# A SwiGLU kernel with its steady block written out in a new order

## The chip, the cores and the metric

The kernel runs on one core of a Trainium2 chip. The metric is the device time of one execution in microseconds (us). A core has TensorE for matrix products (PE in the profile, its weight loads PEld), VectorE (DVE), ScalarE (ACT), GpSimd (POOL) and SyncE (SP), which here only issues DMA transfers. Each engine works through its own instructions in the order in which the program wrote them; an instruction that waits holds up all that stands behind it on its engine.

## The reference

The input is x, 8 sequences of 4096 tokens with 192 channels. It goes through a causal convolution with 7 taps, whose weights are a softmax per head (8 heads of 24 channels), and then through a normalised SwiGLU layer with 1536 hidden channels. Cut to what matters:

```python
w = np.exp(w - np.max(w, axis=-1, keepdims=True))          # weight: 8 heads x 7 taps
w = w / (np.sum(w, axis=-1, keepdims=True) + 1e-09)
out = np.einsum('hk,bskhg->bshg', w, x_unf)                # x_unf: the 7 last tokens
rms = np.sqrt(np.mean(x * x, axis=-1, keepdims=True) + 1e-06)
xn = x / rms * rms_g                                       # x: 32768 tokens x 192
g = xn @ w_gate                                            # 192 x 1536
silu = g * (1.0 / (1.0 + np.exp(-g)))
val = xn @ w_val                                           # 192 x 1536
return (silu * val @ w_out).astype(np.float32)             # 1536 x 192
```

## The kernel before

**Blocks.** The 32768 tokens are cut into 32 pairs of two groups of 512 tokens. The first two pairs are computed with plain products while the weights are still being prepared. Pairs 2 to 31 use a scheme of seven sums and products in place of eight products (Strassen's, in the form of Winograd), both for the gate and value products and for the output product. One steady block of the program is one such pair. It is written out by hand: there is no planner, and no loop decides an order.

**The lists.** The tuple LINE gives the order of the work on TensorE in a block: 68 products, then 42 output steps. The tuple ORDER gives, for the blocks 3 to 32, what all engines do: a word `pN` takes the next N entries of LINE, and each other word adds one instruction (or a few) to the engine of its first letter (A is ACT, V is DVE, G is POOL, S a DMA on the queue of SP). `-` behind a word means the pair before, `+` the next pair, `++` the one after that. SECOND is the same for pair 2, beside which pair 1 ends. FIRST is the same for pair 1; in it `W` takes the next turn of the weight preparation and `R` starts the ring of weights. The function `run` at the end of the kernel reads the words, `Pair.do` and `ahead` write the instructions.

**A product** (`Pair.product`, line 948) multiplies a weight piece with the normalised tokens or with sums of them. Numbers are split into three parts, and a product is six matrix instructions: three parts, each for the gate (first bank of a bank pair) and the value (second bank). The names are P1 to P7, Q1 to Q4 and A, B, E with a letter, then a point and a number j from 0 to 5, which says which sixth of the hidden channels is meant. The even and odd j do not have the same form: 0, 2, 4 and 5 use P and Q words, 1 and 3 use A, B and E words for four quarters a, b, c, d and no sums. The weight pieces lie in DRAM and stream through a ring of 12 slots: when the last product that uses a slot has been issued, the next load into it is put on the queue of SP (`ring_load`, line 822).

**Banks.** Four bank pairs of the accumulator memory (PSUM) are shared by all. For the j of the P and Q form, the scheme gathers the quarters in this order: P1, Q1 and P2 make quarter a; `f1.j` (ACT, line 705) copies a to the bank pair of b; P6, P7, Q3 and P4 add to it to give b; P5 opens the bank pair of c, `f3.j` (ACT, line 705) copies c to a place in the on-chip memory (tt), and `f4.j` and `f5.j` (DVE, line 1025) write the sums for c and d, to which P3, Q2 and Q4 add. So a product can stand behind a copy: P6 or P7 behind f1, P7 or Q3 behind f4 or f5, and a product that opens a bank pair behind the instruction that gives that pair free. For j = 5 (the constant APART) Q4.5 opens the fourth bank pair itself, and `f5.5` and `f6.5` (DVE, line 1018) add from it and from b. For each quarter, `ga.j` to `gd.j` (ACT, line 1031) take the silu of the gate, and `ma.j` to `md.j` (DVE, line 1038) multiply it with the value into the tiles ht; after that the bank pair is free.

**Hidden sums and output steps.** `h1.j` to `h4.j` (line 1003, on DVE as `Vh` or POOL as `Gh`) form the sums over the four quarters; h1 goes into hs, the others overwrite quarters in ht. An output step `oK.j` (`Pair.step`, line 976) multiplies one of these with form K of the output weights, in twelve small matrix instructions, gathered in bank pairs named X, Y and Z. `c1`, `s7` and `c2` (ACT, line 705) copy gathered results, `C22` and `C21` (DVE, line 1055) add them, `T11`, `T12`, `T21` and `T22` (DVE, line 991) transpose the four results into the tile o_sb, and `st` (SP, line 1087) stores it. The steps of form 3 stand behind C22, since they go on in the bank pair that C22 reads; the bank pairs of an old block come free with T11, T12 and C21, and the next block's first products open them.

**What a block does for later blocks.** `ld` loads tokens (line 174), `cv0` (ACT, line 470) and `cv1` to `cv6` (DVE, line 474, called taps here) are the convolution, `sq` squares (ACT, line 485), `red` sums over channels (DVE, lines 496 to 498), `pow` makes the factor (POOL, lines 503 to 509), `bc` spreads it (DVE, line 516), `mul` scales the tokens (POOL, line 524), `pl` puts them away to DRAM (line 1098), `ft` fetches them back transposed (line 676). `x1` to `x4` (line 868) are sums of the tokens, and `n`, `l` and `d` (lines 705, 856, 854) are the three parts of an operand.

**The preparation of weights** runs beside pair 1. `prepare(o)`, for ten kinds o of weight, is a row of stages: a difference (POOL, line 785), the high part (DVE, 788), a scaled copy (ACT, 793), the middle part that reads the copy (DVE, 795), a difference (POOL, 799), the last part (ACT, 801) and the store to DRAM (SP, 805). `turn_of(o, n)` says which o take their next stage in turn n; the turns are sorted by `45 * o + at` with a fixed list of at.

The lines that say how a word moves TensorE on, and when a slot of the ring is filled anew:

```python
if word[0] == "p":
    for _ in range(int(word[1:].rstrip("+-"))):
        if p in pairs:
            next(pairs[p].line)
...
left_of[key] -= 1
if left_of[key] == 0:
    ring_load(slot)
```

Of the kernel before, what the change touches and what calls it, by code (L numbers as in the profile page):

```python
# [20 lines left out]
def kernel(  # L21
# [58 lines left out]
    )  # L80
    ORDER = (
# [15 lines left out]
    )  # L97
    SECOND = (
# [15 lines left out]
    )  # L114
    FIRST = (
# [14 lines left out]
    )  # L130
    LINE = (
# [7 lines left out]
    )  # L139

    cst = ctx.enter_context(tc.tile_pool(name="cst", bufs=1))
# [1127 lines left out]

    def turn_of(o, n):  # L1270
        mine = (
            [o] * (o < 2), [o] * 2 * (o == 0), [o + 1, o, o + 1], [o, o + 2], [o], [o],
        )[n]
        for o in mine:
            if o < NW:
                next(makers[o], None)

    ready = iter([functools.partial(turn_of, o, n) for _, o, n in steps])
    put(base - 1, lambda: outer(first_hts, base))
    put(base + 445, functools.partial(next, pieces["t"], None))  # L1280
# [74 lines left out]
```

## Time and profile before

| what | before |
|---|---|
| median of 3 runs | 2460.54 us (2460.39 to 2461.25) |
| profiled execution | 2460.79 us |
| its span, first to last instruction | 2459.0 us |
| granted clock of TensorE | 1.000 |
| busy: PE, PEld | 2442.9 us (99%), 1886.5 us (77%) |
| busy: DVE, ACT, POOL | 2125.0 us (86%), 1024.3 us (42%), 487.9 us (20%) |
| DMA | 430.55 MB, mean 175 GB/s |

The span is counted from the first instruction to the last, and the profiled execution's own time is 1.8 us longer. Busy times are those of each engine alone. The chain is followed back from the last instruction, at each step to what released it. In a timeline, a row has the start, the duration, the engine, the line, the operation, what it writes and reads, its shape and the number of instructions that the row gathers; a bracket tells how long the engine was idle before and what released it. A row of the windows has, in this order, the stretch, its length, and the busy time with the number of instructions of PE, PEld, DVE, ACT and POOL, then the granted clock, the busy share of the DMA engines and their GB/s; where the row is that of one line, the first two numbers are PE and PEld of that line. A row of the waits has the engine, the line, who released it, the waiting time in all, how often, and the longest.

### The profile page before, as it was taken

To read this page: it belongs to the slowest core of one execution; us is meant where nothing else is said; L and a number is where in the kernel's file an instruction comes from. 1 tells how busy PE (TensorE), PEld (TensorE's weight loads), DVE (VectorE), ACT (ScalarE), POOL (GpSimd) and SP (SyncE) were. 2 spreads that over 40 slices of the span, in tenths; PEclk is the share of its full clock that TensorE was granted. 3 is DMA by queue.
4 is the path that set the end of the run, shared out by engine and by line. 5 is a ranking of instruction groups with operands and counts; after the bars stand their busy time and mean duration, and the time that the engine had idled before them with its cause. 6 is when DMAs were issued, how large, how long until landed. Compare 5 with 4: busy or idle time off the path is not lost.

```text
span 2459.0 us, 69164 instructions
## 1 busy us (share of the span) xinstructions
PE 2442.9 (99%) x29136; PEld 1886.5 (77%) x29136; DVE 2125.0 (86%) x2762; ACT 1024.3 (42%) x1431; POOL 487.9 (20%) x422
## 2 busy tenths in 40 slices
PE   8999999999999999999999999999999999999998
PEld 5647777877777777777777778777777777777776
DVE  8678888899888898888898888998888988888975
ACT  6443344443344443444443444433444434344432
POOL 0542222210222201222202222102222012222021
PEclk9999999999999999999999999999999999999999
DMA  7374778666777667777677786667776766776753
GB/s 152 61 213 125 178 182 212 186 166 168 177 192 206 169 176 175 178 201 200 157 176 176 179 214 184 168 168 180 187 209 168 178 175 178 197 201 160 177 162 92
DMA packets 716392, 430.55 MB, mean 175 GB/s; under 512 B 510330, under 2 KB 702386, under 8 KB 716082
## 3 DMA queue, kind: packets, MB, share of 16 engines
q1 hardware_dynamic: 712336, 425.21, 67.1%
q8 instruction: 230, 3.77, 0.7%
q10 hardware_dynamic: 3746, 0.92, 0.2%
q14 instruction: 80, 0.66, 0.1%
HBM read 366.96 MB, written 58.98 MB: 173 GB/s over the span
## 4 chain that ended last, share of the span: by engine, by line
PE 96%; DMA 1%; DVE 1%; SPq 1%; POOL 0%; ACT 0%; issue 0%; DVEq 0%; ACTq 0%; POOLq 0%
PE ps L948 58%; PE ps L976 36%; PE ps L1135 2%; PE ps L920 1%; DMA ht<-in_moe_w_val_dram 0%; DMA wd<-part 0%; SPq L174 0%; DMA x<-in_x_dram 0%; DVE part L795 0%; POOL part L799 0%; DMA ht<-in_moe_w_gate_dram 0%; DVE ht L1038 0%; SPq L258 0%; DVE ht L1003 0%; DVE part L788 0%
## 5 line engine op out<-in xcount | busy, mean ns | idle before, releaser
L948 PE MATMUL ps<-part,ring 64*128 64x512 f32 x11190 | 1322.7, 389 | 1.8 <-DVE o_sb L991 0.8
L948 PEld LDWEIGHTS ps<-part,ring 64*128 64x128 f32 x11190 | 1039.9, 184 | 250.8 <-DVE ps L1025 22.5
L1031 ACT ACTIVATE tt<-ps 128x512 f32<-128x512 f32 x744 | 438.6, 598 | 659.0 <-PE ps L948 472.8
L1038 DVE TENSOR_TENSOR ht<-ps,tt 128x512 f32<-128x512 f32 x744 | 501.7, 684 | 99.9 <-ACT tt L1031 98.4
L976 PE MATMUL ps<-ht,wo_sb 128*32 128x384 f32 (+2 forms) x7272 | 462.6, 380 | 0.0
L976 PE MATMUL ps<-ht,x 128*32 128x256 f32 (+2 forms) x6696 | 431.7, 379 | 0.0
L1003 POOL TENSOR_TENSOR hs<-ht 128x512 f32<-128x512 f32 x120 | 154.8, 1290 | 1270.6 <-DVE ht L1038 1270.6
L976 PEld LDWEIGHTS ps<-ht,wo_sb 128*32 128x32 f32 x7272 | 330.8, 110 | 98.0 <-DVE ps L1018 10.6
L976 PEld LDWEIGHTS ps<-ht,x 128*32 128x32 f32 x6696 | 299.0, 110 | 87.0
L1025 DVE TENSOR_TENSOR ps<-ps,tt 128x1024 f32<-128x1024 f32 x210 | 258.7, 1232 | 109.0 <-PE ps L948 88.1
L474 DVE SCALAR_TENSOR_TENSOR y<-xh,tp,y 128x1536 f32<-128x1536 f32 x186 | 337.5, 1815 | 1.6 <-ACT y L470 1.3
L705 ACT COPY tt<-ps 128x384 f32<-128x384 f32 (+1 forms) x182 | 151.6, 833 | 260.2 <-PE ps L976 230.5
L1003 DVE TENSOR_TENSOR ht<-ht 128x512 f32<-128x512 f32 x282 | 193.4, 704 | 22.6 <-PE ps L976 22.3
L705 ACT COPY ps<-ps 128x1024 f32<-128x1024 f32 (+1 forms) x151 | 134.0, 887 | 160.6 <-PE ps L976 106.7
L705 ACT CAST part<-tt 128x1024 fp32r<-128x1024 f32 x60 | 63.0, 1049 | 238.0 <-DVE tt L868 238.0
L1003 DVE TENSOR_TENSOR ht<-hs,ht 128x512 f32<-128x512 f32 x181 | 125.3, 693 | 23.8 <-PE ps L976 21.7
L976 PE MATMUL ps<-hs,x 128*32 128x128 f32 (+2 forms) x2232 | 131.6, 379 | 0.0
L976 PEld LDWEIGHTS ps<-hs,x 128*32 128x32 f32 x2232 | 96.5, 110 | 28.7
L948 PE MATMUL ps<-part,part 64*128 64x512 f32 x822 | 116.9, 388 | 0.0
L1003 POOL TENSOR_TENSOR ht<-ht 128x512 f32<-128x512 f32 x90 | 115.1, 1291 | 0.0
L503 POOL TENSOR_SCALAR r<-r 128x8 f32<-128x8 f32 x31 | 6.1, 197 | 524.6 <-DVE r L498 524.4
L856 DVE SCALAR_TENSOR_TENSOR part<-part,xb 128x1024 fp32r<-128x1024 f32 x87 | 106.1, 1219 | 0.0
(137 smaller groups left out, 1582.3 us busy)
## 6 DMA issues: line engine op xcount, KB each, us to landing
ring<-wd SPq DMA_DIRECT2D x1317, 192.0 KB
xb<-xd SPq DMA_DIRECT2D x60, 512.0 KB
part<-wd SPq DMA_DIRECT2D x123, 192.0 KB
xd<-xh SPq DMA_DIRECT2D x240, 96.0 KB
xh<-in_x_dram SPq DMA_DIRECT2D x192, 105.0 KB
xb<-xd SPq DMA_DIRECT2D x60, 256.0 KB
out_dram<-o_sb SPq DMA_DIRECT2D x126, 96.0 KB
out_dram<-o_sb SPq DMA_DIRECT2D x62, 128.0 KB
```

Source lines behind the costliest of these rows:

```text
L474: nc.vector.scalar_tensor_tensor(out=y, in0=xk, scalar=w, in1=y, op0=ALU.mult, op1=ALU.add)
L503: nc.gpsimd.tensor_scalar(out=r, in0=r, scalar1=s / D, scalar2=s * 1e-6, op0=ALU.mult, op1=ALU.add)
L705: nc.scalar.copy(out=dst, in_=src)
L856: nc.vector.scalar_tensor_tensor(out=split_of(g, 2).bitcast(F32R), in0=high, scalar=1.0 + SPLIT, in1=src, op0=ALU.mult, op1=ALU.subtract,)
L920: nc.tensor.matmul(out=self.both(j, c)[:, h, :], lhsT=wf[HALF[h], k, 2 * HOME[j] + f, :], rhs=rb[HALF[h], k, g, :], start=(k == 0), stop=( ...
L948: nc.tensor.matmul(out=self.both(j, c)[:, h, :], lhsT=left[HALF[h]], rhs=right[HALF[h]], start=(first and q == 0), stop=True, skip_group_c ...
L976: nc.tensor.matmul(out=self.acc(b)[i * Q : (i + 1) * Q, at : at + n], lhsT=left, rhs=cols, start=fresh, stop=True, skip_group_check=True, ...
L1003: engine[eng].tensor_tensor(out=dst, in0=a, in1=b, op=op)
L1025: nc.vector.tensor_tensor(out=self.both(j, c), in0=self.both(j, "b"), in1=s5, op=ALU.add)
L1031: nc.scalar.activation(out=tt[:, t, :], in_=self.both(j, c)[:, 0, :], func=AF.Silu)
L1038: nc.vector.tensor_tensor(out=self.hv(j, "abcd".index(c)), in0=self.both(j, c)[:, 1, :], in1=tt[:, t, :], op=ALU.mult,)
L1135: nc.tensor.matmul(out=bank(h, bks[h])[:], lhsT=wf[HALF[h], AT[h][k], u * NF + f, :], rhs=xb[HALF[h], g, k, :], start=(k == 0), stop=(k == ...
```

## The change

ORDER, SECOND and LINE are written anew; the words themselves are the same, so each block has the same products, steps, copies, sums, taps, stores and loads, with one exception: of the sums h POOL does five a block instead of seven (h1.0, h3.0, h1.4, h1.3 and h3.4, before h1.1, h1.2, h3.0, h1.3, h3.2, h3.3 and h1.4), and DVE does the others. Among what moves: Q4.5, which opens the fourth bank pair d, now stands ahead of P7.5; P5.0 moves from place 8 of LINE to 9, P1.2 from 24 to 23, P1.5 from 56 to 55, P5.5 from 57 to 58, P7.5 from 62 to 63, Q3.5 from 67 to 66 (places counted from 0); Q3.2 keeps place 37 and Q4.2 goes from 39 to 36, ahead of it. T11, C21, T22, T21, d.4 and cv0 stand at the end of a block, where before they stood at the start of the next one, with a `-`. The taps cv1 to cv6 stand at other places. In SECOND the six steps of form 3 of pair 1 that are left come in one run (`p6-`) instead of three, two and one. In FIRST cv0 stands ahead of two casts, and `Vl.2+` at its end is gone, for which SECOND begins with `Vl.2`. In `turn_of` the second stage that turn 2 gives to o + 1 goes to turn 4: this is the scaled copy of line 793.

```diff
     ORDER = (
-        "VT11- p1- VC21- p1 Acv0+ p1 Vl.4 VT21- Af1.0 p4 VT22- p1 VT12- Aga.1 Vcv1+ p1 Vma.1",
-        "Vcv3+ p2 Aga.0 Af3.0 p1 Vma.0 Vd.4 p1 Sst0.2- Vf4.0 Agb.1 p2 Agd.1 p1 Vmb.1 p2 Agc.0",
-        "p1 Vcv4+ Vmd.1 Sst1.1- p1 Vf5.0 Vmc.0 Sst0.0- p1 Vcv6+ p1 Agd.0 Vmd.0 p2 Agc.3 p1",
-        "Vmc.3 Agb.0 Vmb.0 p2 Vcv2+ Af1.2 p2 Agc.1 p1 Af3.2 p2 Vmc.1 Sst1.4- Vf4.2 Vcv5+ p1",
-        "Sst1.3- Aga.2 Vma.2 p2 Vf5.2 Asq+ p3 Vh1.0 p1 Agc.2 p1 Agb.3 p1 Vmc.2 p1 Vmb.3 Agb.2",
-        "p1 Sst0.3- p1 Gh1.1 Vmb.2 Agd.2 Af1.4 p1 Vmd.2 p1 Aga.3 Af3.4 Sst0.1- p1 Vred+ p2",
-        "Vma.3 p1 Gpow+ Vf4.4 Vbc+ p4 Aga.4 Gmul+ Spl.4+ p1 Agc.4 Agd.3 Spl.1+ Spl.0+ Gh1.2",
-        "Spl.2+ Gh3.0 Vma.4 Vf5.4 Spl.3+ Vmc.4 Spl.5+ p1 Agd.4 Spl.6+ Vmd.3 p2 Vmd.4 p1 Af1.5",
-        "Sft.0+ Spl.7+ p1 Af3.5 p2 Agb.4 p1 Vf4.5 p1 Sft.2+ Vmb.4 Vf5.5 p1 Aga.5 p1 Vma.5",
-        "Vf6.5 p1 Sft.5+ p3 Agd.5 Agb.5 p2 Vmd.5 Sld.7++ p2 Vh3.1 Gh1.3 p1 Gh3.2 Vmb.5 Ac1",
-        "Gh3.3 Gh1.4 Vh2.1 Sst1.0- An.0+ Agc.5 p4 Vh1.5 p1 Sft.4+ p2 Vh2.3 Sld.5++ Sld.3++",
-        "Vh3.4 Sld.1++ Vh2.2 Vh3.5 p1 Vh2.5 Vmc.5 Vl.0+ p2 Vh2.0 Vx3+ Sld.4++ p2 Sld.0++ Vx1+",
-        "p1 Vh2.4 p2 Vx2+ As7 p1 Vd.0+ p1 Vh4.4 p2 Sld.6++ Vh4.2 An.3+ Sst1.2- An.1+ p1 Ac2",
-        "p2 Vh4.1 Vh4.5 p2 Vl.1+ Vd.3+ p1 Vl.3+ p1 An.2+ Vd.2+ Sld.2++ Sst0.4- Vh4.3 p3 VC22",
-        "p1 Vl.2+ p1 Vh4.0 p1 Vd.1+ Vx4+ p3 An.4+",
+        "p1 Vcv5+ p1 VT12- p1 Af1.0 p2 Vcv4+ p2 Aga.1 Vcv6+ p1 Vma.1 p1 Aga.0 p1 Agb.1 Vma.0",
+        "p2 Vl.4 p1 Vmb.1 Af3.0 p1 Vf4.0 Vcv1+ Agd.1 Sst1.1- p1 Vmd.1 p2 Vf5.0 Sst1.2- p1",
+        "Agc.0 p2 Agc.3 Vcv3+ Sst0.2- p2 Vmc.0 Vmc.3 p2 Vh1.1 p1 Agb.0 p1 Vmb.0 Agd.0 Vmd.0",
+        "Af1.2 Vcv2+ p2 Agc.1 Vmc.1 Af3.2 p2 Sst0.1- p1 Aga.2 p1 Vf4.2 p2 Asq+ p1 Vma.2 Vf5.2",
+        "Sst1.4- Vred+ Agc.2 Gpow+ p1 Sst1.3- p3 Vmc.2 p1 Agd.2 Agb.2 Agb.3 Vmd.2 Vmb.3 p3",
+        "Vmb.2 Af1.4 p1 Gh1.0 Aga.3 Vbc+ p1 Af3.4 p3 Gmul+ Aga.4 Vma.3 p1 Spl.1+ Vf4.4 Vma.4",
+        "p5 Agc.4 Spl.0+ Spl.7+ Vf5.4 Spl.2+ Vmc.4 Spl.4+ Agd.3 Spl.5+ Spl.3+ Vh3.1 p1 Gh3.0",
+        "Vmd.3 p1 Spl.6+ Agd.4 p1 Sft.0+ Sft.2+ Vmd.4 Vh1.2 p1 Af1.5 p1 Agb.4 Vmb.4 p2 Af3.5",
+        "p1 Vf4.5 p2 Vf5.5 Aga.5 Vma.5 p1 Gh1.4 p2 Sft.4+ Vf6.5 Vh3.2 Agd.5 Gh1.3 p1 Agb.5",
+        "Vh3.3 p1 Vh2.0 p5 Vmd.5 Vmb.5 Ac1 Sft.5+ Vh1.5 Agc.5 p1 An.0+ Sst0.4- p1 Vh3.5",
+        "Sst0.0- Vh2.2 Sld.5++ Gh3.4 p1 Vh2.1 Vh2.4 Sld.1++ p1 Sld.7++ p1 Vh2.5 p2 Sst0.3-",
+        "Vl.0+ Vd.0+ Sst1.0- p2 Vmc.5 p1 Vx1+ As7 Sld.3++ p2 Sld.2++ An.1+ Vx2+ p4 Sld.0++",
+        "Vh4.2 Vh2.3 Vh4.5 Vx4+ p1 Vh4.1 p1 Sld.4++ An.3+ p1 Vd.1+ Vl.3+ p2 Vl.1+ Sld.6++",
+        "Vd.3+ Ac2 Vh4.3 An.2+ Vl.2+ p2 Vh4.0 p1 Vh4.4 p4 Vd.2+ VC22 p2 VT11 p2 Vx3+ VC21",
+        "An.4+ p2 Acv0++ VT22 VT21 p1 Vd.4+ p1",
     )
     SECOND = (
-        "p1 VC22- VT11- p1 p1- Vl.4 p2- Af1.0 p1 VT22- p1 VT21- p2 p2- p1 p1- Aga.1 VT12- p1",
-        "Vma.1 Vcv3+ p2 Aga.0 Af3.0 p1 Vma.0 Vd.4 p1 Vf4.0 Sst0.4- Agb.1 Sst0.2- p1 Sst1.4-",
-        "p1 Agd.1 p1 Vmb.1 p2 Agc.0 p1 Vcv4+ Vmd.1 p1 Vf5.0 Vmc.0 p1 Vcv6+ p1 Agd.0 Vmd.0 p2",
...
+        "p2 Vl.2 VC22- VT11- p6- Vd.4 VT22- VT21- VT12- Vcv5+ p1 Af1.0 p2 Vcv4+ p2 Aga.1",
+        "Vcv6+ Sst0.4- Sst0.2- Sst1.4- p1 Vma.1 p1 Aga.0 p1 Agb.1 Vma.0 p2 Vl.4 p1 Vmb.1",
+        "Af3.0 p1 Vf4.0 Agd.1 p1 Vmd.1 p2 Vf5.0 p1 Agc.0 p2 Agc.3 Vcv3+ p2 Vmc.0 Vmc.3 p2",
+        "Vh1.1 p1 Agb.0 p1 Vmb.0 Agd.0 Sst0.3- Vmd.0 Af1.2 Sst1.1- p2 Agc.1 Sst0.0- Vmc.1",
...
     )
...
-        "Ac1 Sld.3++ Vh3.5 Vh2.5 Sld.4++ Sld.5++ Sld.6++ Sld.7++ An.0+ An.4+ Gl.0+ Vd.0+ p4",
-        "Vh4.5 p1 Vh4.0 R p3 As7 p6 Ac2 Acv0++ Vcv1++ Vcv2++ Vh4.3 p8 Vh4.2 p2 Vh4.1 p2 VC21",
-        "p1 Vh4.4 Vl.2+",
+        "Ac1 Sld.3++ Vh3.5 Vh2.5 Sld.4++ Sld.5++ Sld.6++ Sld.7++ Acv0++ An.0+ An.4+ Gl.0+",
+        "Vd.0+ p4 Vh4.5 p1 Vh4.0 R p3 As7 p6 Ac2 Vh4.3 Vcv1++ Vcv2++ p8 Vh4.2 p2 Vh4.1 p2",
+        "VC21 p1 Vh4.4",
...
     LINE = (
-        "P1.0 Aa.1 Ea.1 Ba.1 P2.0 P6.0 Q1.0 Ab.1 P5.0 Bb.1 Eb.1 Ad.1 Bd.1 Ed.1 Q2.0 P3.0 P7.0",
-        "Ac.3 Ec.3 Bc.3 Q4.0 Ac.1 P4.0 Q3.0 P1.2 Ec.1 Bc.1 P5.2 P6.2 Q1.2 P2.2 Ab.3 Eb.3 P7.2",
-        "Q2.2 P3.2 Bb.3 Q3.2 P4.2 Q4.2 P1.4 Aa.3 Ea.3 Ba.3 P5.4 P6.4 Q1.4 P2.4 Ad.3 Bd.3 P7.4",
-        "Q2.4 P3.4 Ed.3 Q4.4 P4.4 P1.5 P5.5 Q3.4 P6.5 P2.5 Q1.5 P7.5 Q2.5 Q4.5 P3.5 P4.5 Q3.5",
-        "o1.4 o1.5 o1.1 o1.2 o1.0 o1.3 o7.2 o7.0 o7.3 o2.3 o7.1 o2.0 o6.1 o2.4 o6.5 o7.4 o2.1",
-        "o6.2 o7.5 o6.3 o6.0 o2.2 o2.5 o6.4 o4.5 o4.3 o5.5 o5.1 o5.4 o5.3 o5.2 o5.0 o4.4 o4.0",
-        "o4.1 o3.5 o3.2 o3.1 o4.2 o3.4 o3.0 o3.3",
+        "P1.0 Aa.1 Ba.1 Ea.1 Ab.1 P2.0 Q1.0 Eb.1 Bb.1 P5.0 P6.0 Ad.1 Bd.1 Ed.1 Ac.3 P7.0 P3.0",
+        "Q2.0 Ec.3 Bc.3 Q3.0 Q4.0 P4.0 P1.2 Ac.1 Ec.1 Bc.1 P5.2 P6.2 P2.2 Q1.2 Ab.3 P7.2 P3.2",
+        "Q2.2 Bb.3 Q4.2 Q3.2 P4.2 Eb.3 P1.4 Aa.3 Ea.3 Ba.3 P5.4 P6.4 P2.4 Q1.4 Ad.3 P7.4 Q2.4",
+        "P3.4 Ed.3 Bd.3 Q4.4 P1.5 Q3.4 P4.4 P5.5 P6.5 Q1.5 P2.5 Q4.5 P7.5 P3.5 Q2.5 Q3.5 P4.5",
+        "o1.0 o1.5 o1.3 o1.2 o1.4 o1.1 o7.1 o7.3 o2.2 o7.4 o7.5 o6.0 o6.4 o6.5 o7.0 o7.2 o2.5",
+        "o6.2 o2.1 o2.0 o4.1 o6.1 o4.2 o4.0 o6.3 o4.5 o2.3 o2.4 o5.1 o5.0 o5.4 o5.2 o5.5 o5.3",
+        "o4.3 o4.4 o3.4 o3.2 o3.0 o3.1 o3.5 o3.3",
     )
...
     def turn_of(o, n):
         mine = (
-            [o] * (o < 2), [o] * 2 * (o == 0), [o + 1, o, o + 1], [o, o + 2], [o], [o],
+            [o] * (o < 2), [o] * 2 * (o == 0), [o + 1, o], [o, o + 2], [o + 1, o], [o],
         )[n]
```

The rest of SECOND is, word for word nearly, the new ORDER without the stores of the pair before.

23 rows, old and new, of the table SECOND are left out of this document.

## Prediction

> **What bounds the kernel now.** I read the page first, then the windows of one steady block, the waits, and the timeline of each engine around the places where TensorE waits.
>
> ```profile
> span 2459.0 us, 69164 instructions
> PE 2442.9 (99%) x29136; PEld 1886.5 (77%) x29136; DVE 2125.0 (86%) x2762; ACT 1024.3 (42%) x1431; POOL 487.9 (20%) x422
> PE 96%; DMA 1%; DVE 1%; SPq 1%; POOL 0%; ACT 0%; issue 0%; DVEq 0%; ACTq 0%; POOLq 0%
> ```
> ```profile
> 289.82 42.73 PE ps L948 x372
> 364.37 42.74 PE ps L948 x372
> ...
> 2378.07 42.52 PE ps L948 x372
> ```
>
> TensorE carries 96% of the chain. A steady block starts every 74.57 us (2378.07 - 289.82 is 28 blocks). What such a block consists of:
>
> ```profile
> 1408.58:1483.15 74.57, 74.53 (x914) 58.92 (x913) 66.03 (x85) 31.05 (x43) 13.94 (x12) 1.00 0.70 182
> 1408.58:1455.71 47.13, 47.09 (x408) 37.91 (x408) 1.00 0.71 196
> 1455.71:1483.15 27.44, 27.44 (x504) 21.00 (x504) 1.00 0.68 159
> ```
> ```profile
> 1436.81 6.96 PE L948 MATMUL ps<-part,ring 64*128 64x512 f32 x60
> 1443.61 0.84 PE L948 MATMUL ps<-part,part 64*128 64x512 f32 x6
> ...
> 1483.15 0.96 PE L948 MATMUL ps<-part 64*128 64x512 f32 x6
> 1483.95 6.29 PE L948 MATMUL ps<-part,ring 64*128 64x512 f32 x54
> ```
>
> The second and third window rows are L948 and L976 alone: 68 products, then 42 output steps, at the full clock. Ten products take 1443.61 - 1436.81 = 6.80 us, so one takes 0.680 and 68 take 46.24; the first of a block takes 0.80, 0.12 more, for the change of kind. The product stage therefore loses 47.13 - 46.24 - 0.12 = 0.77 us. Who makes it wait:
>
> ```profile
> PEld ps L948 <- DVE ps L1025: 23.8, 60, 0.5
> PEld ps L948 <- ACT ps L705: 7.7, 30, 0.3
> POOL hs L1003 <- DVE ht L1038: 1270.6, 61, 41.8
> ACT part L793 <- DVE part L795: 15.5, 7, 4.1
> SPq L822 <- PE ps L948: 813.1, 1005, 18.6
> ```
> ```profile
> 1433.95 1.92 PEld L948 LDWEIGHTS ps<-part,ring 64*128 64x128 f32 x18 [0.34 <-DVE ps L1025]
> ...
> 1449.04 1.90 PEld L948 LDWEIGHTS ps<-part,ring 64*128 64x128 f32 x18 [0.26 <-ACT ps L705]
> 1451.40 3.96 PEld L948 LDWEIGHTS ps<-part,ring 64*128 64x128 f32 x36 [0.46 <-DVE ps L1025]
> ```
>
> Three places per block. Counting 0.680 a product from 1408.58 + 0.12, Q3.2 (37 products in) was due at 1433.86, P6.5 at 1449.03 and P7.5 at 1451.19, the losses before each added. P6.5's load came at its due time and still cost 0.11 (the load no longer hides), so a load that is t late costs t + 0.11: 0.20, 0.12 and 0.32, 0.64 together; 0.03 for the products just behind them makes 0.67. The other 0.1 is the change to output steps, which stays. **0.67 us of 74.57 is all that an order can win in the steady part.**
>
> **The change part by part.** The block keeps its 68 products and 42 steps; two of its seven h sums on POOL go to DVE. Durations:
>
> ```profile
> 1427.96 1.01 ACT L705 COPY tt<-ps 128x1024 f32<-128x1024 f32 x1
> 1429.01 1.23 DVE L1025 TENSOR_TENSOR ps<-ps,tt 128x1024 f32<-128x1024 f32 x1
> 1430.15 1.81 DVE L474 SCALAR_TENSOR_TENSOR y<-xh,tp,y 128x1536 f32<-128x1536 f32 x1
> ...
> 1450.12 1.23 DVE L1025 TENSOR_TENSOR ps<-ps,tt 128x1024 f32<-128x1024 f32 x1 [2.21 <-PE ps L948]
> 1452.41 1.23 DVE L1018 TENSOR_TENSOR tt<-ps,tt 128x1024 f32<-128x1024 f32 x1 [0.47 <-PE ps L948]
> 1465.44 1.29 DVE L868 TENSOR_TENSOR tt<-xb 128x512 f32<-128x512 f32 x2
> 1473.22 1.22 DVE L856 SCALAR_TENSOR_TENSOR part<-part,tt 128x1024 fp32r<-128x1024 f32 x1
> 1474.35 1.22 DVE L854 TENSOR_TENSOR part<-tt,part 128x1024 fp32r<-128x1024 f32 x1
> 1477.22 0.55 DVE L1055 TENSOR_TENSOR tt<-ps,tt 128x384 f32<-128x384 f32 x1
> ```
>
> An instruction that need not wait starts about 0.08 before the one in front ends (1473.22 to 1474.35 is 1.13): I count 0.60 for a 512 wide DVE operation, 1.135 for a 1024 wide one, 1.73 for a tap (L474), 0.47 for C22.
>
> *The three waits go.* Q3.2 waited for f5.2, held up by the tap at 1430.15; the new list has no tap between f4.2 and f5.2. There f5.2 follows ma.2, whose silu needs Q1.2 (30 products in): 20.40, 0.90 to the silu (as from P5.2 to f3.2, 1427.96 - 1427.06), the silu 0.60, 0.03, ma.2's 0.69 (684 ns in the page's groups) and 0.10 is 22.72, its end 23.95, with 0.16 for the load 24.11, against 24.48 for Q4.2, now the first reader. P6.5 gets four products behind P1.5 (2.72) instead of three, where f1.5 needs 0.95 to start, 1.00 like the copy in the rows above and 0.16 for the load, 2.11. P7.5 needs f3.5, then f4.5, behind P5.5: by the f3.2 and f4.2 rows (P5.2, 27 products in, started at 1408.58 + 0.12 + 18.36 = 1427.06) 0.90 + 1.05 + 1.23 + 0.16 = 3.34 us, and has five products, 3.40. All three go: **0.67 back**. P7.2 and P7.4, which had six products, get the same five, so 0.06 is left there too.
>
> *Q3.5 waits.* f5.5 started 0.90 after P7.5 did (1452.41 against 1451.40 + 0.11). Its first reader was four products behind P7.5 (2.72); now Q3.5 is three behind, 2.04. Needed: 0.90 + 1.23 + 0.16 = 2.29. **0.25 lost.**
>
> *o3.4 waits for C22.* From f5.5 to C22 DVE hardly waits in the new list: 23 operations of 0.60, 10 of 1.135, three waits for a result just made (0.12 each, my estimate), and C22 itself with 0.55: 13.85 + 11.35 + 0.36 + 0.55 = 26.11; with 0.90 before and 0.15 behind, 27.16 us after P7.5 started. TensorE arrives after five products (3.40), the 0.25, 0.11 for the change and 36 steps of 0.648 (27.44 less 0.20 over 42): 27.09. **0.07 lost.** A longer wait at Q3.5 shortens this one; together about 0.32.
>
> *Ties.* From C22 the same DVE run goes on through transposes, x3, d.4 and three taps to ma.1 for P5.0 (10.99 after C22 starts, where TensorE takes 11.04) and to mc.0 for P1.2 (0.07 to spare). Between nothing and 0.1 each; I take **0.05** in all, because the sums leave a margin. Another 0.01 for products behind a wait. Net 0.67 - 0.25 - 0.07 - 0.05 - 0.01 = **0.29 per block, 8.1 us over 28 blocks.**
>
> *The other queues.* On SP stores, put-aways and fetches change places among the ring loads; no TensorE row names a DMA as its releaser in the steady part, and SP waits 813 us for products to free slots, so I cost this at nothing (bounds: nothing, and 4 us once if a load came late). POOL scales (L524) at much the same point of the block and has two sums fewer; its longest wait, 41.8 us, covers that. ACT's cv0 stands at the end of a block instead of the start of the next, the same place in its queue.
>
> *Second pair.* Its six leftover steps now run in one go.
>
> ```profile
> 208.46 1.66 PE L948 MATMUL ps<-part,ring 64*128 64x512 f32 x12
> 210.05 2.16 PE L976 MATMUL ps<-ht,wo_sb 128*32 128x384 f32 x36
> 219.10 3.40 PE L948 MATMUL ps<-part,ring 64*128 64x512 f32 x25 [0.80 <-DVE o_sb L991]
> ```
>
> The steps can start at 210.05 as before (C22 of the first pair), end at 213.94, and Ba.1 starts at 214.27. The transpose that frees a bank, then three taps now ahead of ma.1, put ma.1 at 214.24 + 0.54 + 3 x 1.73 + 0.2 = 220.2 and P5.0, which waits for it, at 221.05, where TensorE alone would be at 219.03. From there to the next block are 74.28 - 6.13 = 68.15, so that starts at 289.2 instead of 289.75: two changes of kind and the 0.80 saved, 2.0 paid. **0.55 won.**
>
> *Scaled copy.*
>
> ```profile
> 164.81 0.63 ACT L793 ACTIVATE part<-part 128x512 f32<-128x512 f32 x1 [3.90 <-DVE part L795]
> 165.34 0.58 ACT L1031 ACTIVATE tt<-ps 128x512 f32<-128x512 f32 x1
> 166.70 1.56 PE L920 MATMUL ps<-xb,part 64*128 64x512 f32 x6 [0.73 <-DVE ht L1038]
> ```
>
> The copy waited 3.90 us for DVE with a silu behind it, and TensorE waited 0.73 for that silu's bank. Moved later, it stands behind the silu. What is late next is L795 on DVE, which reads the copy. Between 0.9 won (0.73 with a hidden load) and 0.9 lost; I take **0.6 won**, since the copy's reader comes only two to three turns behind its new place. cv0 ahead of two casts in the first pair's end: between nothing and its own 1.6 us; nothing, as the steps running there do not read them. The last block has no Q3.2 wait to lose, and gains 0.15.
>
> Sum: 8.1 + 0.55 + 0.6 + 0.15 = 9.4. The profiled execution took 2460.79 (span 2459.0 and 1.8 around it), 0.25 over the median 2460.54; from the median, **2451.1 us**.
>
> **Rivals.** *No change: the short windows cost.* P7.2, P7.4 and P7.5 have 0.06 us to spare. If ACT or DVE hands over 0.17 later than at f4.2, each loses 0.11, 0.33 a block. For it: f3 shares ACT with silus. Against: the f3.2 row is itself such a hand-over. Then 28 x 0.04 is lost and 1.3 won: 2460.3.
>
> *Slower: POOL and DVE meet.* Beside POOL's L524, a DVE sum took far longer than its mean of 704 ns:
>
> ```profile
> 137.38 3.17 DVE L1003 TENSOR_TENSOR ht<-ht 128x512 f32<-128x512 f32 x1
> 136.76 3.31 POOL L524 TENSOR_TENSOR xh<-y,s 128x1536 f32<-128x1536 f32 x1
> L1003 DVE TENSOR_TENSOR ht<-ht 128x512 f32<-128x512 f32 x282 | 193.4, 704 | 22.6 <-PE ps L976 22.3
> L1003 POOL TENSOR_TENSOR hs<-ht 128x512 f32<-128x512 f32 x120 | 154.8, 1290 | 1270.6 <-DVE ht L1038 1270.6
> ```
>
> In the new list POOL makes h1.4, h1.3 and h3.4 from 41.1 us of the block, three times 1.27, until 44.9; DVE starts h3.2 at 46.6. If POOL is 1.7 us late, they meet, inside the run to C22, which has no room. At a third of that excess, 0.8 a block: 28 x (0.8 - 0.29) = 14.3 lost, 1.3 won: 2473.5. Against: the mean of 704 over 282 sums says that they rarely meet now. [...]
>
> *More: the run to C22 is hidden and Q3.5 costs nothing,* if reads overlap more than counted: 0.67 x 28 + 1.3: 2440.5. Against: the f5.5 row.
>
> **Numbers.** Forecast 0.66 (its own range 2447 to 2455.5, 0.13 to 0.43 a block), no change 0.15, slower 0.13, more 0.06. About 0.2%, 4.9 us, is what a measurement can tell here. Faster 0.72, same 0.15, slower 0.13. The range 2446 to 2464 holds the first two.
>
> **What would show it.** No wait at Q3.2's, P6.5's or P7.5's place; one at Q3.5, released by L1018, of about 0.3 in the weight loads; a small one at an output step released by DVE L1055; blocks of 74.28; one wait near 219 us for DVE L1038; none at 166.7. The prediction is wrong if L1003 on DVE has a mean above 0.75, if P7.2 waits, or if DVE's idle time before C22 is gone and o3.4 waits over 0.4.

## The result and the profile after

The changed kernel takes 2451.45 us (median of 6 runs, 2450.83 to 2453.5), the kernel before, beside it, 2460.79 us (2460.39 to 2461.25). The ratio is 0.9964, with a 95% interval of 0.9953 to 0.9975: 9.3 us less, where 9.4 were forecast. The sum came out nearly exactly, but that is partly luck: two of its terms are far off, as the table below shows.

Of the page of the changed kernel, the span, the busy times and the chain:

```profile
span 2449.5 us, 69165 instructions
PE 2434.2 (99%) x29136; PEld 1907.2 (78%) x29136; DVE 2165.7 (88%) x2822; ACT 1027.2 (42%) x1431; POOL 412.3 (17%) x362
PE 96%; DMA 1%; DVE 1%; SPq 1%; POOL 1%; ACT 0%; issue 0%; DVEq 0%; POOLq 0%
```

The rows of its chain at which a steady block begins (start, us, what), and the windows of one block, whole, products alone (line 948) and steps alone (line 976):

```profile
289.05 46.89 PE ps L948 x404
...
1403.67 46.86 PE ps L948 x408
1477.97 46.86 PE ps L948 x408
...
2369.84 46.83 PE ps L948 x408
```
```profile
1403.67:1477.97 74.30, 74.30 (x915) 58.66 (x914) 67.32 (x87) 31.24 (x42) 11.42 (x10) 1.00 0.71 183
1403.67:1450.53 46.86, 46.86 (x408) 37.99 (x408) 1.00 0.71 203
1450.53:1477.97 27.44, 27.44 (x504) 20.54 (x504) 1.00 0.70 149
```

The chain no longer breaks inside a block: it is one piece of 408 matrix instructions. A block takes 74.30 us; from 289.05 to 2369.84 are 28 blocks of 74.31, against 74.58 before (2378.07 - 289.82). The steps take 27.44 as before, and all of the gain is among the products: 46.86 instead of 47.13. What weight loads waited for, first over the whole run, then in this block:

```profile
PEld ps L948 <- DVE tt L1018: 11.3, 30, 0.4
PEld ps L948 <- DVE ht L1038: 2.6, 2, 2.2
PEld ps L976 <- DVE tt L1055: 0.4, 1, 0.4
```
```profile
1403.60 6.01 PEld L948 LDWEIGHTS ps<-part,ring 64*128 64x128 f32 x54 [0.20 <-issue]
1448.86 1.24 PEld L948 LDWEIGHTS ps<-part,ring 64*128 64x128 f32 x12 [0.37 <-DVE tt L1018]
```

The waits of product loads for line 1025 and for the copy of line 705 (60 and 30 times before) are gone, and the one that was forecast at Q3.5 stands in each block, released by f5.5. Where the 9.5 us between the two spans (2459.0 and 2449.5) went, by the first matrix instruction of each block in the timelines of both (the chain's rows begin 0.07 us later):

| stretch | before | after | won | forecast |
|---|---|---|---|---|
| to the first product of pair 2 | 208.46 | 208.37 | 0.09 | 0.6 |
| pair 2 | 81.29 | 80.61 | 0.68 | 0.55 |
| 28 steady blocks | 2088.25 | 2080.79 | 7.46 | 8.1 |
| last block and stores | 81.00 | 79.73 | 1.27 | 0.15 |

### The profile page after: what moved, and what is told of

It reads as the page before. It is cut to its first block, busy times and chain, and to the rows that moved or that the text cites. A ratio compares the mean times of both kernels' runs of the same rounds, so it can differ in the third digit from the quotient of the medians.

```text
span 2449.5 us, 69165 instructions
## 1 busy us (share of the span) xinstructions
PE 2434.2 (99%) x29136; PEld 1907.2 (78%) x29136; DVE 2165.7 (88%) x2822; ACT 1027.2 (42%) x1431; POOL 412.3 (17%) x362
## 4 chain that ended last, share of the span: by engine, by line
PE 96%; DMA 1%; DVE 1%; SPq 1%; POOL 1%; ACT 0%; issue 0%; DVEq 0%; POOLq 0%
PE ps L948 57%; PE ps L976 36%; PE ps L1135 2%; PE ps L920 1%; DMA ht<-in_moe_w_val_dram 0%; DMA wd<-part 0%; POOL part L799 0%; SPq L174 0%; DMA x<-in_x_dram 0%; DVE y L474 0%; DVE part L795 0%; DMA ht<-in_moe_w_gate_dram 0%; SPq L258 0%; DVE ht L1003 0%; DVE ht L1038 0%
## 5 line engine op out<-in xcount | busy, mean ns | idle before, releaser
L948 PEld LDWEIGHTS ps<-part,ring 64*128 64x128 f32 x11304 | 1081.3, 184 | 215.5 <-DVE tt L1018 11.3
L976 PE MATMUL ps<-ht,wo_sb 128*32 128x384 f32 (+2 forms) x7272 | 443.8, 380 | 0.0
L976 PE MATMUL ps<-ht,x 128*32 128x256 f32 (+2 forms) x6696 | 405.1, 379 | 0.0
L976 PEld LDWEIGHTS ps<-ht,wo_sb 128*32 128x32 f32 x7272 | 311.4, 110 | 103.3 <-issue 11.6
L976 PEld LDWEIGHTS ps<-ht,x 128*32 128x32 f32 x6696 | 287.6, 110 | 95.0 <-POOL ht L1003 0.2
L1003 DVE TENSOR_TENSOR ht<-ht 128x512 f32<-128x512 f32 x312 | 213.7, 702 | 10.3 <-PE ps L976 9.2
L1003 POOL TENSOR_TENSOR hs<-ht 128x512 f32<-128x512 f32 x90 | 115.6, 1298 | 275.2 <-DVE ht L1038 227.9
L1003 DVE TENSOR_TENSOR ht<-hs,ht 128x512 f32<-128x512 f32 x181 | 117.4, 689 | 0.1
L854 DVE TENSOR_TENSOR part<-xb,part 128x1024 fp32r<-128x1024 f32 x87 | 105.9, 1218 | 0.0
L948 PE MATMUL ps<-part,part 64*128 64x512 f32 x720 | 103.3, 387 | 0.0
```

The lines of the kernel that those rows point to most:

```text
L854: e.tensor_tensor(out=split_of(g, 1).bitcast(F32R), in0=src, in1=high, op=ALU.subtract)
L948: nc.tensor.matmul(out=self.both(j, c)[:, h, :], lhsT=left[HALF[h]], rhs=right[HALF[h]], start=(first and q == 0), stop=True, skip_group_c ...
L976: nc.tensor.matmul(out=self.acc(b)[i * Q : (i + 1) * Q, at : at + n], lhsT=left, rhs=cols, start=fresh, stop=True, skip_group_check=True, ...
L1003: engine[eng].tensor_tensor(out=dst, in0=a, in1=b, op=op)
```

## The experiments

### Why Q3.2 waited

```diff
-Vmc.1 Sst1.4- Vf4.2 Vcv5+ p1 Sst1.3- Aga.2 Vma.2 p2 Vf5.2 Asq+
+Vmc.1 Sst1.4- Vf4.2 p1 Sst1.3- Aga.2 Vma.2 p2 Vf5.2 Vcv5+ Asq+
```

> The kernel before, with the tap cv5 moved from between f4.2 and f5.2 to just behind f5.2; nothing else. If the tap was what made Q3.2 wait, the 0.20 us go in 28 blocks: 5.6 us less, 2455.2 us, steady blocks of 74.37 us, and no weight load that waits 25 us into a block, while the waits at P6.5 and P7.5 (0.12 and 0.32 us) stay. If f5.2 is late because ma.2 or its silu is late, the tap is no cause: 2460.8 us and Q3.2 waits as before. If the moved tap makes something behind it late (h1.0, mc.2, the square), a new wait appears before product 45 and the gain is smaller than 5.6 us.

Measured: 2510.9 us (2509.88 to 2511.87), 50 us more. The wait 25 us into a block is gone, as forecast, but a block takes 76.3 us. Waits over the whole run, then ACT and TensorE in one block:

```profile
ACT xh L485 <- DVE y L474: 125.3, 29, 4.4
PE ps L948 <- DVE ht L1038: 47.4, 28, 1.7
```
```profile
1384.77 1.49 ACT L485 ACTIVATE xh<-y 128x1536 f32<-128x1536 f32 x1 [4.43 <-DVE y L474]
1386.17 2.04 ACT L1031 ACTIVATE tt<-ps 128x512 f32<-128x512 f32 x4
```
```profile
1387.52 4.83 PE L948 MATMUL ps<-part,ring 64*128 64x512 f32 x40 [1.69 <-DVE ht L1038]
```

The square reads the last tap and stands in ACT's queue ahead of four silus. With the tap later it waits 4.43 us (1.4 at most before), the silus behind it are late, and P1.4 waits 1.69 us for the bank pair that one of their products frees. So the tap did make Q3.2 wait; that wait of 0.20 us was the price of a square that did not hold up ACT. In the changed kernel the last tap, cv2, stands ahead of f3.2, well before the square.

### Why P6.5 waited

```diff
-Q4.4 P4.4 P1.5 P5.5
+Q4.4 P1.5 P4.4 P5.5
```

> The kernel before, with P1.5 ahead of P4.4; nothing else. P6.5 then stands four products behind P1.5, as in the changed kernel. The prediction took the place behind P1.5 as the cause of the 0.12 us at P6.5: then they go in 29 blocks, 3.5 us less, 2457.3 us. In the trace of before, though, the copy f1.5 waited 0.81 us for DVE (md.4, which frees the bank pair into which it copies), not for P1.5. If that is the cause, the wait at P6.5 stays, 2460.8 us, and the cure in the changed kernel was that md.4 comes sooner.

Measured: 2467.89 us (2467.22 to 2468.62), 7.1 us more. Neither of the two: the weight loads' waits for line 1038 went from 0.8 us in all to

```profile
PEld ps L948 <- DVE ht L1038: 15.2, 33, 0.5
```

P1.5 itself opens a bank pair, and one place earlier this was not yet free: P1.5 came 0.22 us late and the product behind it another 0.12. P6.5's wait of 0.12 went, and a block takes 74.81 us, 0.23 more than before.

This run does not part the two causes, since P6.5 itself came 0.35 us later. DVE and ACT in the kernel before say more:

```profile
1445.80 2.10 DVE L1038 TENSOR_TENSOR ht<-ps,tt 128x512 f32<-128x512 f32 x3 [0.76 <-ACT tt L1031]
1447.99 1.00 ACT L705 COPY ps<-ps 128x1024 f32<-128x1024 f32 x1 [0.81 <-DVE ht L1038]
```

The last of the three multiplications on DVE, md.4, ends at 1447.90 us, and the last matrix instruction of P1.5 at 1447.85: the copy f1.5 stood behind both, 0.05 us apart. In the changed kernel, too, f1.5 starts 0.99 us behind P1.5 (1441.25 to 1442.24), as before (1447.01 to 1447.99). What is new is that P6.5 stands one product further on. So the place behind P1.5 counts, as long as DVE gives its bank pair free in time; a run that moves one of the two alone was not made.

### The place of Q4.5

```diff
-P2.5 Q4.5 P7.5 P3.5 Q2.5 Q3.5
+P2.5 P7.5 Q4.5 P3.5 Q2.5 Q3.5
```

> The changed kernel, with Q4.5 behind P7.5 again; nothing else. P7.5 then stands four products behind P5.5 (2.72 us), where f3.5 and f4.5 need 3.34 us: P7.5 waits 0.62 us, 0.7 us with a load that no longer hides. Q3.5 then stands four products behind P7.5 and its 0.25 us go. Net 0.4 to 0.5 us more a block in 29 blocks, 12 to 14 us: 2463 to 2466 us, with the wait at P7.5 released by line 1025 and none by line 1018. If five products are more than f3.5 and f4.5 need, so that the place of Q4.5 does not matter for P7.5, the 0.25 us at Q3.5 are won and it takes 2444 us.

Measured: 2461.25 us (2458.88 to 2462.22), 9.8 us more than the changed kernel. Waits of weight loads and of TensorE:

```profile
PEld ps L948 <- DVE ps L1025: 22.8, 30, 0.8
PE ps L948 <- DVE ps L1025: 10.1, 30, 0.3
```

In a block P7.5 starts 0.50 us late and the product behind it another 0.12, 0.62 in all, and the wait for line 1018 at Q3.5 is gone. The 0.62 is 3.34 less 2.72: of the 0.16 us that the sum has for the load, some 0.05 lie between the end of f4.5 and the load, and the rest is about the 0.12 lost behind it, so the 0.7 of the expectation counted this part twice. The net is smaller than expected, 0.28 a block over 28 blocks (74.59 against 74.31): some of the small delays of 0.01 to 0.02 us went, too. This one swap, which the change made in the other direction, is worth as much as the whole gain in the steady part. The steady blocks explain 7.9 of the 9.8 us.

### Can Q3.5's wait be had as well?

```diff
-P1.5 Q3.4 P4.4 P5.5 P6.5 Q1.5 P2.5 Q4.5 P7.5 P3.5
+P1.5 Q3.4 P5.5 P4.4 P6.5 Q1.5 P2.5 P7.5 Q4.5 P3.5
-Vmd.4 Vh1.2 p1 Af1.5 p1 Agb.4 Vmb.4 p2 Af3.5 p1 Vf4.5 p2 Vf5.5 Aga.5 Vma.5 p1 Gh1.4
+Vmd.4 Vh1.2 Af1.5 p1 Af3.5 p1 Agb.4 p2 Vf4.5 Vmb.4 p1 p1 Vf5.5 Aga.5 Vma.5 p1 p1 Gh1.4
```

> The changed kernel, with P5.5 ahead of P4.4 and P7.5 ahead of Q4.5, and f3.5 and f4.5 ahead of the silu and the product of b.4, which stand one product later; nothing else. P7.5 stays five products behind P5.5, and Q3.5 stands four behind P7.5: its wait of 0.25 us goes. P5.5 opens the bank pair that md.4 gives free 0.2 to 0.4 us too late for the earlier place. If this bank sets it, the block loses 0.4 to 0.5 us there and wins 0.25: 2455 to 2458 us, with a new wait for line 1038 some 39 us into the block. If the bank is free in time, 2444.5 us.

The same moves stand in SECOND. Measured: 2467.35 us (2465.8 to 2468.68), 15.9 us more than the changed kernel:

```profile
PEld ps L948 <- DVE ht L1038: 21.3, 49, 2.2
PEld ps L948 <- DVE ps L1025: 13.7, 30, 0.5
```

Q3.5 waits no more and P5.5 with the product behind it loses 0.39 us for the bank pair of md.4, as expected, but P7.5 loses another 0.32 us behind f4.5, which was not. DVE's timeline has why:

```profile
1380.07 1.23 DVE L1025 TENSOR_TENSOR ps<-ps,tt 128x1024 f32<-128x1024 f32 x1 [1.90 <-PE ps L948]
```

f4.5 waited for TensorE and not for the copy f3.5. It adds from b, to which P6.5 still has to add, and P6.5 stands only three products ahead of P7.5 here. The block is 0.47 us longer, 13.1 us over 28 blocks; Q3.5's wait is the cheaper one. Another 1.6 us of this profiled execution lie in the second pair, where TensorE's granted clock was 0.57 from 221 to 225 us and single products took up to 1.28 us instead of 0.68; this comes up again at the tie below.

### The second pair

```diff
-p2 Vl.2 VC22- VT11- p6- Vd.4 VT22- VT21- VT12- Vcv5+ p1 Af1.0 p2 Vcv4+ p2 Aga.1
+p2 Vl.2 VC22- VT11- p3- Vd.4 VT22- VT21- p1 Af1.0 p2- p1 p1- VT12- Vcv5+ p1 Vcv4+ p2 Aga.1
```

> The changed kernel, with the six leftover steps of pair 1 in the second pair's list in three runs again (three, two and one, a product between them) instead of one run; nothing else. In the changed kernel the chain that sets P5.0 near 221 us is the last of these steps, then the transpose T12, three taps and ma.1. Two products (1.36 us) and two more changes of kind and back (0.66 us) ahead of the last step then move the whole chain by 2.0 us: the third pair starts 2.0 us later (291.0 us), 2453.4 us. If only the changes of kind count, as the prediction had it, 0.7 us more, 2452.1 us. If the wait at P5.0 hides it, 2451.4 us.

Measured: 2453.94 us (2452.69 to 2454.76), 2.5 us more; the third pair starts at 291.17 us, against 288.98 in the changed kernel's timeline. T12 starts at 216.31 us there and ma.1 at 222.28, each 2.2 us later than in the rows below: the chain through T12 set it, not the changes of kind alone. The chain in the changed kernel, DVE and then TensorE (both timelines):

```profile
214.14 0.65 DVE L991 STREAM_TRANSPOSE o_sb<-ps 128x256 f32<-128x256 f32 x2 [1.76 <-PE ps L976]
214.71 5.49 DVE L474 SCALAR_TENSOR_TENSOR y<-xh,tp,y 128x1536 f32<-128x1536 f32 x3
220.12 1.28 DVE L1038 TENSOR_TENSOR ht<-ps,tt 128x512 f32<-128x512 f32 x2
```
```profile
220.85 3.70 PE L948 MATMUL ps<-part,ring 64*128 64x512 f32 x30 [1.80 <-DVE ht L1038]
```

Three taps stand between the transpose and ma.1, which frees the bank pair for P5.0. Two of them have other places, those that cv1 and cv2 have in the steady list:

```diff
-VT12- Vcv5+ p1 Af1.0 p2 Vcv4+ p2 Aga.1 Vcv6+ ... Vf4.0 Agd.1 ... Vmd.0 Af1.2
+VT12- Vcv5+ p1 Af1.0 p2 p2 Aga.1 ... Vf4.0 Vcv4+ Agd.1 ... Vmd.0 Af1.2 Vcv6+
```

> The changed kernel, with two taps of the second pair's list moved: cv4 from ahead of ma.1 to behind f4.0, cv6 from ahead of ma.1 to behind md.0; nothing else. If the three taps ahead of ma.1 are what makes P5.0 wait 1.8 us near 219 us, ma.1 ends 3.5 us sooner, the wait goes, and the third pair starts 1.8 us sooner (287.2 us instead of 289.0): 2449.6 us. If the transpose behind the last step is what sets ma.1, the wait stays and it takes 2451.4 us. If the taps make something late at their new places, a new wait appears in the second pair, and less is won.

Measured: 2448.29 us (2448.14 to 2448.68), ratio to the kernel before 0.9948 (0.9936 to 0.9961). In its profiled execution the second pair takes 78.6 us instead of 80.6 and TensorE does not wait:

```profile
213.69 8.46 PE L948 MATMUL ps<-part,ring 64*128 64x512 f32 x72
```

The second pair gave 2.0 us; that the medians differ by 3.2 is not all explained (0.3 us lie ahead of pair 2 and 0.8 in the steady blocks, in the profiled executions of both, which is no more than single executions differ by).

### The tie at P5.0

```diff
-Aga.1 Vcv6+ p1 Vma.1
+Aga.1 p1 Vma.1 Vcv6+
```

> The changed kernel, with the tap cv6 moved from ahead of ma.1 to behind it in the steady list; nothing else. The prediction counted a tie there: ma.1 ends 0.05 us before P5.0 needs its bank, and in one block of the profiled execution P5.0 waited 0.24 us. If the two of six executions of the changed kernel that took 2 us more lost that tie in more blocks, this kernel has no execution above 2452 us, and a median of 2451.2 us. If they come from elsewhere, its executions spread as those of the changed kernel did (2450.8 to 2453.5 us).

Measured: 2451.7 us (2450.34 to 2452.8). The executions spread as before the move; the tie at P5.0 is not their cause. The traces show another candidate. In two of them, that of the exchange for Q3.5 above and that of the sums on POOL below, TensorE's granted clock fell to 0.5 for 3.41 us (from 221.44 and from 223.02 us), just behind the 1.8 us for which P5.0 waits in the second pair, and that pair took 1.6 us longer: with the sums on POOL the same 354 matrix instructions of the chain behind the wait took 42.37 us, in the changed kernel 40.76. The other five profiled executions with this wait show no such fall, nor do the seven without it. The two kernels with the taps of the second pair moved have no such wait, and their executions spread least (0.5 and 1.0 us). That this clock makes the 2 us in the changed kernel is not shown, since no execution of it that took 2 us more has a trace. Both moves together:

> The changed kernel with both moves: the taps cv4 and cv6 of the second pair's list, and the tap cv6 of the steady list. If the two moves do not touch each other, 1.8 us less than the changed kernel and no execution that is 2 us longer: 2449.4 us. This is the version that is meant to beat both kernels.

Measured: 2448.24 us (2448.01 to 2448.97), ratio 0.9948 (0.9936 to 0.9961). It beats both kernels, but so does the move in the second pair alone, by the same.

### The end

```diff
-o4.1 o3.5 o3.2 o3.1 o4.2 o3.4 o3.0 o3.3
+o4.1 o4.2 o3.5 o3.2 o3.1 o3.4 o3.0 o3.3
```

> The kernel before, with the step o4.2 moved from between the last steps of form 3 to ahead of o3.5; nothing else. In the changed kernel the last block ended 1.2 us sooner behind its last transpose (from 2452.92 to 2459.0 before, from 2444.60 to 2449.5 after). If that is because the steps of form 4 are done before those of form 3, so that C21, T22 and T21 and five of the ten last stores are out before the last steps end, then this kernel gains about 1.2 us at its end and nothing else: 2459.6 us. If the last five stores alone set the end, nothing changes: 2460.8 us. The steady blocks stay at 74.57 us in both cases.

Measured: 2459.39 us (2458.93 to 2460.22), against 2460.84 of the kernel before beside it (2460.2 to 2462.18, 21 runs): 1.45 us less by medians. The interval of the ratio (0.9986 to 1.0003) holds no change, too, so the traces count. The timeline of the end, before, and below it this kernel:

```profile
2451.11 1.16 DVE L991 STREAM_TRANSPOSE o_sb<-tt 128x256 f32<-128x256 f32 x4
2452.11 4.20 ACTq L1087 DMA_DIRECT2D out_dram<-o_sb  x6
2452.30 1.87 SPq L1087 DMA_DIRECT2D out_dram<-o_sb  x4
2452.47 0.65 DVE L991 STREAM_TRANSPOSE o_sb<-ps 128x256 f32<-128x256 f32 x2 [0.20 <-PE ps L976]
```
```profile
2449.79 1.16 DVE L991 STREAM_TRANSPOSE o_sb<-tt 128x256 f32<-128x256 f32 x4
2450.79 4.97 ACTq L1087 DMA_DIRECT2D out_dram<-o_sb  x6
2450.97 3.59 SPq L1087 DMA_DIRECT2D out_dram<-o_sb  x4
2453.10 0.65 DVE L991 STREAM_TRANSPOSE o_sb<-ps 128x256 f32<-128x256 f32 x2 [2.15 <-PE ps L976]
```

Before, all ten last stores were issued from 0.4 us ahead of the last transpose on. Here those of T22 and T21 leave 2.3 us ahead of the last transpose, and from its start (2453.10) to the end (2458.4) are 5.3 us instead of 6.5. In the changed kernel it is 5.3, too (2444.15 to 2449.5). Its steady blocks were 74.61 us here, no faster than before.

### The scaled copy

```diff
-[o + 1, o, o + 1], [o, o + 2], [o], [o],
+[o + 1, o], [o, o + 2], [o + 1, o], [o],
```

> The kernel before, with only turn_of changed as in the changed kernel (the scaled copy of line 793 two turns later). By the prediction 0.6 us less, 2460.2 us, and no wait at 166.7 us. By the trace of the changed kernel, where the wait came back in two parts (0.2 us at 162.7 and 0.45 us at 168.2), about 0.3 us less by 185 us and 0.1 us less by the start of the second pair, 2460.7 us. If the copy, now later, holds up line 795 and so the stores of the weights, the second pair starts later than 208.46 us.

Measured: 2460.41 us (2459.91 to 2461.39), against 2460.84.

> The changed kernel, with turn_of as it was before. By the prediction 0.6 us more than the changed kernel, 2452.0 us, with a wait of 0.7 us near 166.7 us. If the scaled copy is worth only what is left of it at the start of the second pair, 0.1 us more, 2451.5 us, the second pair starting at 208.5 us; the steady blocks stay at 74.30 us in both cases.

Measured: 2450.96 us (2450.46 to 2453.68), against 2451.45. Added to before it seems to win 0.4 us, taken from the changed kernel it seems to win 0.5: it is worth nothing that these runs can tell. TensorE with the late copy (the kernel before with the copy moved), and without (the changed kernel with the copy moved back):

```profile
168.76 15.72 PE L920 MATMUL ps<-xb,part 64*128 64x512 f32 x72 [0.30 <-DVE ht L1038]
```
```profile
166.62 18.30 PE L920 MATMUL ps<-xb,part 64*128 64x512 f32 x84 [0.72 <-DVE ht L1038]
```

The wait did not go; it moved to the next silu. This one stands behind the last part (line 801), which waits for a difference on POOL, 1.26 us in the kernel before with the copy moved, and in the changed kernel:

```profile
166.93 0.84 ACT L801 ACTIVATE part<-part 128x768 fp32r<-128x768 f32 x1 [1.27 <-POOL part L799]
```

By 185 us 0.5 us had been won in the kernel before with the copy moved. A step's load then waited 0.36 us for a sum on POOL, at 195.12 us, and 0.2 were left at the start of pair 2 (208.25 us, 208.46 before). In the changed kernel pair 2 starts at 208.37 us with the late copy and at 208.38 without.

### POOL and DVE side by side

```diff
-Vh3.3 p1 Vh2.0 ... Sst0.0- Vh2.2 Sld.5++ Gh3.4 p1 Vh2.1 Vh2.4
+Vh3.3 p1 Gh2.0 ... Sst0.0- Gh2.2 Sld.5++ Gh3.4 p1 Gh2.1 Vh2.4
```

> The changed kernel, with the sums h2.0, h2.2 and h2.1 of the steady list on POOL instead of DVE; nothing else. POOL then sums from 41.3 to 49 us of the block and DVE makes h3.2 and h3.3 beside it, from 46.9 us. If POOL and DVE disturb each other at such sums, as the prediction's rival had it, DVE's sums (line 1003) there take over 1.0 us instead of 0.7, and POOL's over 1.3. If they do not, both keep their durations, DVE has 1.8 us more room ahead of C22 and P5.0, the small losses there go, and it takes 2449 to 2451.4 us.

Measured: 2493.65 us (2491.89 to 2495.44), 42 us more. POOL, then DVE, in one block:

```profile
1400.79 1.36 POOL L1003 TENSOR_TENSOR ht<-hs,ht 128x512 f32<-128x512 f32 x1 [4.07 <-PE ps L976]
1402.66 1.43 POOL L1003 TENSOR_TENSOR ht<-hs,ht 128x512 f32<-128x512 f32 x1 [0.51 <-PE ps L976]
1404.05 1.73 POOL L1003 TENSOR_TENSOR ht<-ht 128x512 f32<-128x512 f32 x1
1405.73 1.28 POOL L1003 TENSOR_TENSOR ht<-hs,ht 128x512 f32<-128x512 f32 x1
```
```profile
1399.73 1.28 DVE L1003 TENSOR_TENSOR ht<-ht 128x512 f32<-128x512 f32 x2
1400.93 1.28 DVE L1038 TENSOR_TENSOR ht<-ps,tt 128x512 f32<-128x512 f32 x2
1402.98 1.66 DVE L1003 TENSOR_TENSOR ht<-ht 128x512 f32<-128x512 f32 x1
1405.81 2.36 DVE L1003 TENSOR_TENSOR ht<-hs,ht 128x512 f32<-128x512 f32 x2 [1.18 <-PE ps L976]
1412.29 0.68 DVE L1003 TENSOR_TENSOR ht<-ht 128x512 f32<-128x512 f32 x1
```

In this block a sum on DVE that took 0.68 us alone (at 1412.29 us) took 1.66 beside sums on POOL (at 1402.98), and two, the first of them beside one, took 2.36 where two had taken 1.28 (at 1399.73). POOL's own sums took 1.28 to 1.73 there. The two multiplications at 1400.93 us, which read one operand from PSUM, took 1.28 us together beside POOL's first sum, as two of them did without one (at 220.12 us above). (The sums came later than expected: h2 overwrites what the steps of form 1 read, and POOL waits for these.) The 1.5 us a block have two sources, which this run does not part: the stretched sums, and h3.4, which now stands behind h2.2 in POOL's queue, so that steps and DVE wait for it.

## Why the prediction was right, and where it was not

*The three waits go: right, with one reason that was too simple.* The rows of lines 1025 and 705 are gone. P7.5 needs five products behind P5.5; with four, it and the product behind it lost 0.62 us, which is what 3.34 less 2.72 gives. For Q3.2 the tap was the cause, but it could not simply be moved (the square). For P6.5 the count of products behind P1.5 holds, but the bank pair that DVE frees came within 0.05 us of it and was not in the sum; no run parts the two.

*Q3.5 loses 0.25: right.* The two products there start 0.11 and 0.14 us late, 0.25 in all; the row of the weight loads shows 0.37.

*o3.4 loses 0.07: nothing was lost.* The steps take 27.44 as before. The run from f5.5 to the end of C22 took the 26.11 us of the sum (1447.59 to 1473.70; that 23 operations of 0.60 are 13.80 and not 13.85 did not matter; the 0.12 for a result just made, an estimate there, shows in the changed kernel's trace where x2 reads x1 and starts 0.72 us behind it, 1460.19 to 1460.91, 0.12 more than 0.60). The load of o3.4 came 0.05 us behind that end, at 1473.75, where 0.15 was counted, and no step was late. The one load that waited for line 1055 stands in pair 2, and the kernel before has it, too.

*Ties, 0.06: too small.* The products lose 46.86 - 46.24 - 0.12 - 0.10 = 0.40, of which 0.25 are Q3.5's. The other 0.15 lie in delays of 0.01 to 0.02, most of them about P7.2, P5.0 and P7.5, the windows that had 0.06 or less to spare. With the steps' 0.07 saved the net is 0.27 instead of 0.29.

*Second pair, 0.55: 0.68, with the chain as forecast.* T12 started at 214.14 us, ma.1 at 220.12 and P5.0 at 220.85, where 214.24, 220.2 and 221.05 were forecast. P5.0 came 1.97 us later than TensorE alone would have brought it, against 2.0; the row shows the 1.80 for which TensorE stood idle. What does not add up is the reason behind the 0.55: two changes of kind (0.66) and 0.80 saved with 2.0 paid are a loss. It leaves out the 0.3 that the block itself wins and some 0.8 that the products between 222 and 232 us lost to late loads in the kernel before and lose no more. The 0.55 is right because it is the difference of two starts, which needs no such list.

*Scaled copy, 0.6: at most 0.2.* The bounds of 0.9 either way held it. The step that failed is that the silu's wait would be gone with the copy: the next silu stands behind line 801, which waits for POOL.

*Last block, 0.15: 1.27.* The forecast looked at Q3.2 alone and not at what follows the last product. That the steps of form 4 now precede those of form 3, and thus half the stores leave early, stood in LINE. This error and those of the copy and the steady part cancelled, which is luck: 2451.1 came nearer than its terms.

*The rivals.* "POOL and DVE meet" did not happen: line 1003 on DVE has a mean of 702 ns for the same form as before (704). But such a meeting has its price, as the last experiment shows: there a DVE sum beside sums on POOL took 0.98 us more than one alone (1.66 less 0.68), a little above the 0.8 a block that was assumed. Why they take longer side by side is not shown. "No change" would have needed 0.17 us more at each short window; they lost 0.06 at most in the block shown.

## What to carry to other kernels

Where TensorE is the bound and a block loses some tenths to waits, count for each hand-over how many products stand between the one that starts it and the one that needs it, and compare with the measured time of the hand-over: that gave the 0.62 us that one product too few cost at P7.5. Before moving an instruction out of the way, look for who reads its result and what stands behind that reader in its queue, and which instruction frees the buffer that the moved one needs. And read the end of the run as a stage of its own: half the stores leaving before the last step ended were worth 1.2 us here, as much as four blocks of the gain in the steady part, and can cost one swap.

## What was not expected of the hardware

With three more sums on POOL, a DVE sum that ran beside POOL's took 1.66 us where one alone took 0.68, while POOL's took 1.28 to 1.73, against a mean of 1.29 in the kernel before. In the changed kernel a late weight load was partly hidden at Q3.5: the loads stood idle for 0.37 us by their row, and the products lost 0.25. And in two of the seven profiled executions in which TensorE waited 1.8 us or more for P5.0 in the second pair, its granted clock was 0.5 for 3.41 us just behind that wait.
